# The order of ScalarE and VectorE through the first gate and value tile, written out by hand

## The chip, the cores and the metric

One core of a Trainium2 chip runs the kernel. The metric is the device time of one launch in microseconds: 483.07 us before the change (median of three runs, 482.94 to 483.83). Beside it stands one execution under the profiler, from which all rows below come.

## The reference

Attention with a soft cap over 24 heads, then two feed-forward layers, all in 32-bit floats. The change concerns the last layer, of which only the gate and value products matter here (x has 896 rows of 768 columns, both weights 768 by 1536):

```
def _moe2_ref(x, w_gate, w_val, w_out):
    g = x @ w_gate
    silu = g * (1.0 / (1.0 + np.exp(-g)))
    val = x @ w_val
    return (silu * val @ w_out).astype(np.float32)
```

The inputs arrive as 64-bit floats; the kernel makes 32-bit ones of them on the engines.

## The kernel before

**The work around the change.** The kernel computes attention, then the first feed-forward layer (its last products write the banks x), then the gate and value products, tile by tile of 128 columns of the weights (fc = 0 to 11), and last the output product (banks p). A full product is three matmuls of TensorE (PE): each 32-bit operand is split into a high and a low part, and high·high, high·low and low·high are added up (`mm3`). The helper `split` makes such a pair: ScalarE (ACT) copies the source into the high part (`hi_act`), VectorE (DVE) subtracts that from the source for the low part (`lo_dve`). So every split hands over from ACT to DVE.

**Tile 0** is computed directly by `ff2_gv`: four banks in turn, g and v for the first 384 rows of x, g and v for the other 512, each of 18 matmuls. ACT takes Silu of a g bank into ee, DVE multiplies it by the v bank and the result is split into buffers called a.

**Tiles 1 to 6** are computed by `ff2_gv_seven`, a scheme of Strassen's kind with seven products of half size (nine matmuls each). It needs sums and differences of weight halves and of quarters of x. Those of x are made once: four tiles T[0] to T[3], which the text calls T1 to T4, summed in xf and split into the buffer a (1344 columns each). Those of the weights are made for each tile by the steps that `sum_steps` returns: `sums` (the buffers t and wv), `first` (the split of wg into buffer g4[0], and then two subtractions in wg), `second` (two splits, of wv and t, into g4[2]), `third` (the split of the changed wg into g4[3] or g4[1]) and `fourth` (the split into w). Buffers g4 are called g in the rows, as is the PE's gate bank; 128x768 or 128x384 with source wg, wv or t is a weight buffer. For a tile, PE runs g, (in tile 1 also d), again g into the same bank, b, (c), again b into the same bank, c and e. Before PE adds into g or b again, ACT must have copied the first g product into ee, and DVE must have read the first b.

**The weights** of a tile come by DMA in 64-bit form (wg_raw, wv_raw, issued on SP) and are converted by `f32_shifted`: two ACTIVATEs on ACT, 768 columns each, then one SCALAR_TENSOR_TENSOR on DVE (called shift-and-or in this text). The converted floats wg and wv have two buffers in all, so the conversion for tile 2 waits until the last split of tile 1 has read them. The sums t and wv are made by DVE for tile 1 and by GpSimd (POOL) from tile 2 on.

**What sets the order.** A scheduler places the instructions of each engine, except on engines that stand in `pinned`, whose instructions keep the order in which the program writes them. PE is pinned all along, and ACT in tiles 1 to 6. In tile 0 of the kernel before, DVE is pinned for `sums` and `first`, ACT and DVE for `third`, DVE for what follows the loop (`second`, T3, `fourth`, T4), and ACT for the start of the conversion for tile 2. The rest is placed by the scheduler. On each engine an instruction that waits holds up all behind it.

**Names in the order.** g_2620, d_2635, b_2654, c_2666 and e_2696 are the PE banks of tile 1; g_384 and v_384 are those of tile 0's second half; a_2485 is the buffer of T1 to T4, a_2484 that of the split results of tile 0. wg_2492 and wv_2498 are the converted weights of tile 1. Those of tile 2 are wg_2612 and wv_2618 in the program before, wg_2607 and wv_2613 in the one after.

Of the kernel before, what the change touches and what calls it, by code (L numbers as in the profile page):

```python
# [5 lines left out]
F32 = mybir.dt.float32  # L6
# [4 lines left out]
AF = mybir.ActivationFunctionType  # L11
ALU = mybir.AluOpType
# [25 lines left out]
class Kernel:  # L38
# [562 lines left out]
    def load_gv(self, fc, i):  # L601
# [9 lines left out]
        self.hi_act(d[:, 0], f)  # L611
        self.lo_dve(d[:, 1], f, d[:, 0])

    def ff2_gv(self, fc, N, o):
        nc = self.nc
        ps = []
        for n, w in zip("gv", self.gvs[fc]):
            acc = self.pt.tile([128, 512], F32, name=f"{n}_{fc}_{o}", tag="m")[:, :N]
            for kk in range(self.KD):
                self.mm3(acc, (w[:, 0, kk, :], w[:, 1, kk, :]), [self.x2[kk][:, u, o:o + N] for u in range(2)],  # L620
                         kk == 0, kk == self.KD - 1)
            ps.append(acc)
        sg = self.sg[o > 0]
        self.A.activation(sg, ps[0], AF.Silu)
        first, k = fc < self.KD, fc % self.KD
        if o and first:
            n = self.HN
            self.V.tensor_tensor(self.S1f[:, k], ps[1][:, :n], sg[:, :n], op=ALU.mult)
            self.V.tensor_tensor(sg[:, n:], ps[1][:, n:], sg[:, n:], op=ALU.mult)
            self.V.tensor_tensor(self.S3f[:, k], self.sg[0], self.S1f[:, k], op=ALU.subtract)  # L630
            self.split(self.A61[k], sg[:, n:])
            return
        self.V.tensor_tensor(sg, ps[1], sg, op=ALU.mult)
        if o:
            self.V.tensor_tensor(self.S1f[:, k], self.S1f[:, k], sg[:, :self.HN], op=ALU.add)
        self.split((self.A22 if o else self.A11 if first else self.A12)[k], sg)

    def x_sub(self, t, c, a, z, p, m):

# [27 lines left out]
        self.x_sub(3, c, 384, 448, b[:, :64], t2[:, 384:])  # L667
        self.x_sub(2, c, 0, 448, t2, f)

    def x_split(self, i):  # L670

        self.split([self.T[i][:, u] for u in range(2)], self.xf[:, i])

    def sum_steps(self, fc):

        add, sub = ALU.add, ALU.subtract
        if fc > self.KD + 1:
            return (lambda: None,) * 5
        f = []
        for n, w in zip("gv", (self.w_gate, self.w_val)):  # L680
            src = w[:, fc * 128:(fc + 1) * 128].rearrange("(k p) f -> p k f", p=128)
            f.append(self.f32_shifted(self.load_shifted(src, f"w{n}_{fc}"), f"w{n}_{fc}", n == "v"))
        g, (v, rest) = f
        if fc > self.KD:
            d = [self.g4[m].rearrange("p (u x) -> p u x", u=2) for m in (2, 3)]

            def gate():
                self.split([d[0][:, u] for u in range(2)], g)

            def value():  # L690
                self.split([d[1][:, u] for u in range(2)], v)

            self.gvs[fc] = [t.rearrange("p u (k f) -> p u k f", f=128) for t in d]
            return rest, value, gate, lambda: None, lambda: None
        g, v = (t.rearrange("p (h x) -> p h x", h=2) for t in (g, v))
        s1 = self.t1
        pair = lambda t: [t.rearrange("p (h u x) -> p h u x", h=2, u=2)[:, :, u] for u in range(2)]
        t = self.gvs[fc] = [self.g4[0], self.g4[1 + fc % 2 * 2], self.g4[2], self.w1]
        S = self.G if fc > 1 else self.V

        def sums():
            rest()
            S.tensor_tensor(s1, v[:, 0], v[:, 1], op=add)
            S.tensor_tensor(v[:, 0], g[:, 0], v[:, 0], op=sub)

        def first():
            self.split(pair(t[0]), g)
            self.V.tensor_tensor(g[:, 0], s1, g[:, 0], op=sub)
            self.V.tensor_tensor(g[:, 1], g[:, 1], g[:, 0], op=sub)

        def second():
            hi, lo = pair(t[2])
            for m, x in enumerate((v[:, 0], s1)):
                self.split((hi[:, m], lo[:, m]), x)

        def third():
            self.split(pair(t[1]), g)

        def fourth():
            self.split([self.w1[:, u] for u in range(2)], v[:, 1])  # L720

        return sums, first, second, third, fourth

    def ff2_gv_seven(self, fc, steps):

        V, G, add, mult = self.V, self.G, ALU.add, ALU.mult
        n, k, ee = self.HN, fc % self.KD, self.ee
        a, s24, s31, a22 = self.gvs[fc]
# [10 lines left out]

        sg, c22, p1, u2 = (ee[:, 448 * m:448 * m + 448] for m in range(4))  # L740
        last = fc == self.KD
        sums, first, second, third, fourth = steps
        a = bank("g")
        product(a, A11, X(0, 0), True)
        self.A.activation(p1, a, AF.Copy)
# [1 line left out]
        if fc > 1:  # L747
            self.late()
        if last:
            first()  # L750
        if fc == 1:
            d = bank("d")
            product(d, S4, X(1, 1), True)
# [8 lines left out]
        else:  # L762
            product(a, A12, X(1, 0), False)
        if not last:
            first()
        self.A.activation(sg, a, AF.Silu)
        product(b, S3, T3, False)
        V.tensor_tensor(p1, p1, b, op=add)
# [1 line left out]
            c = bank("c")  # L770
            product(c, S1, T1, True)
        V.tensor_tensor(c22, p1, c, op=add)
        second()
        e = bank("e")
        product(e, A22, T4, True)
        V.tensor_tensor(p1, p1, e, op=add)
        third()
        fourth()
        if fc > 1:
            product(c, S4, X(1, 1), False)  # L780
        V.tensor_tensor(u2, u2, c, op=add)
# [10 lines left out]
        steps = self.sum_steps(fc + 2)  # L792
# [223 lines left out]
    def run(self):  # L1016
        nc = self.nc
        KD, K1, K2, F1 = self.KD, self.K1, self.K2, self.F1
# [16 lines left out]
        w = [self.w_in_steps(i) for i in range(KD)]  # L1035
        f, g, hi, lo = zip(*w)
        self.w_steps = [((), f[0][:1], ()), (f[0][1:2], (), f[0][2:] + g[0][:1]), ((), (g[0][1], hi[0]), (lo[0],))]
        for i in range(1, KD):
            a = g[i][:1]
# [41 lines left out]
        steps = h[1] + h[2][:1] + T[0] + h[2][1:] + h[3][:1] + T[1] + h[3][1:] + wo[0] + h[4][:2] + T[2] + h[4][2:] + wo[1] + h[5][:5] + T3 + h[5][5:] + h[6][:-1] + T4 + h[6][-1:]  # L1081
# [3 lines left out]
        n = self.HN = self.DM // 2  # L1085
        wb, gb = self.pool("wb"), self.pool("gb")
# [6 lines left out]
        steps = x2[0][0] + x2[0][1] + wo[2] + x2[1][0][:1] + T5 + x2[1][0][1:] + x2[1][1] + T6  # L1093
        steps += wo[3] + x2[2][0][:1] + x2[0][2] + x2[1][2] + [(0.0, lambda j=j: self.x_sums0(j)) for j in J[:2]]
        for j in range(2, KD):
# [4 lines left out]
            a, b = x2[j]  # L1100
# [26 lines left out]
        for fc in range(K2):  # L1127
            if 1 <= fc <= KD:
                self.pinned = (nc.tensor, nc.scalar)
                steps = self.ff2_gv_seven(fc, steps)  # L1130
                continue
            self.pinned = (nc.tensor,)
            if fc == KD + 1:
                w8 = self.w8 = wb.tile([128, 8, 2, n], F32R, name="w8", tag="w8")
                w = both(w8) + [(w1[:, 0], w1[:, 1])]
                w += [p for g in self.g4[:2] for p in both(g.rearrange("p (k u n) -> p k u n", k=2, u=2))]
                self.B11, self.B21 = w[4:10], w[:4] + w[10:12]
            for i, (N, o) in enumerate(((n, 0), (512, n))):
                if fc == 0:
                    if i == 0:  # L1140
                        sums, first, second, third, fourth = self.sum_steps(1)
                        self.pinned = (nc.tensor, nc.vector)
                        sums()
                        first()
                        self.pinned = (nc.tensor, nc.vector, nc.scalar)
                        third()
                        self.pinned = (nc.tensor,)
                    else:
                        self.x_split(1)
                        self.x_split(0)  # L1150
                elif fc + 1 < K2:
                    self.load_gv(fc + 1, i)
                elif i == 0:
                    self.load_w2(5)
                    self.load_w2(10)
                for c in early.get(fc, ())[i:i + 1]:
                    self.load_w2(c)
                self.ff2_gv(fc, N, o)
            if fc == 0:
                self.pinned = (nc.tensor, nc.vector)  # L1160
                second()
                self.x_split(2)
                fourth()
                self.x_split(3)
                self.pinned = (nc.tensor, nc.scalar)
                steps = self.sum_steps(2)


        self.pinned = ()
# [42 lines left out]
```

## Time and profile before

| | |
|---|---|
| median of three runs | 483.07 us (482.94 to 483.83) |
| the profiled execution | 480.33 us, its span 478.6 us |
| PE busy | 468.6 us (98%), 2988 matmuls |
| DVE busy | 375.2 us (78%) |
| ACT busy | 307.2 us (64%) |
| POOL busy | 42.8 us (9%) |

The profiled execution is 1.73 us longer than its span, and 2.74 us below the median of the timed runs. Times in rows count from the span's start. Tile 0 runs from 227.5 to 242, tile 1 from 242 to 258, tile 2 from there. A duration in a row overlaps the next row's start by some 0.1 us where instructions of one engine follow each other, so the step from start to start is what an instruction costs in a chain.

### The profile page before, as it was taken

The page shows a single profiled execution, that of the slowest core. Times are in us where ns is not written, and L with a number is a line of the kernel's source. Part 1 is how long each engine was busy: PE and PEld are TensorE (multiplying, and loading weights), DVE is VectorE, ACT ScalarE, POOL GpSimd, SP SyncE. Part 2 cuts the span into 40 slices and gives each one's busy share as a digit, 9 for nine tenths or more (in the row PEclk, how much of TensorE's full clock was granted, in tenths as well). Part 3 has the DMA queues.
Part 4 walks back from the last instruction along what each step waited for, and adds up shares of the span by engine and source line. Part 5 has one row for each costly group of instructions (what it writes and reads, how often), then busy time and mean ns, then how long its engine had stood idle before and what let it go on. Part 6 is the DMA issues. An engine that isn't in the chain of part 4 may idle for free. (4 is left out here: it accounts for less than half of the span.)

```text
span 478.6 us, 7682 instructions
## 1 busy us (share of the span) xinstructions
PE 468.6 (98%) x2988; PEld 386.7 (81%) x2988; DVE 375.2 (78%) x636; ACT 307.2 (64%) x445; POOL 42.8 (9%) x82
## 2 busy tenths in 40 slices
PE   9999999999999999999988999999999999999997
PEld 7445454538888899898977899999998899999996
DVE  3699999987769996765867888878566757999991
ACT  5999999931234798986944666678777746435220
POOL 1020101021000010000011333310000000000000
PEclk9999999999999999999999999999999999999999
DMA  6887575002000316365021444445666642010012
GB/s 179 185 210 165 133 189 147 21 2 88 0 1 12 120 45 198 96 195 167 3 71 62 132 132 131 132 131 162 198 206 213 210 133 66 1 66 2 18 58 90
DMA packets 65061, 52.33 MB, mean 109 GB/s; under 512 B 35585, under 2 KB 61953, under 8 KB 64257
## 3 DMA queue, kind: packets, MB, share of 16 engines
q1 hardware_dynamic: 64992, 51.85, 36.4%
q8 instruction: 23, 0.38, 0.3%
q14 instruction: 14, 0.11, 0.1%
q0 software_dynamic: 32, 0.00, 0.0%
HBM read 49.09 MB, written 2.75 MB: 108 GB/s over the span
## 5 line engine op out<-in xcount | busy, mean ns | idle before, releaser
L30 PE MATMUL g<-x,g 128*128 128x384 f32 (+2 forms) x324 | 69.6, 365 | 4.5 <-ACT ee L30 4.5
L30 PEld LDWEIGHTS g<-x,g 128*128 128x128 f32 x324 | 59.3, 188 | 11.3 <-ACT ee L30 5.3
L30 PE MATMUL h<-wi,x 128*128 128x512 f32 x252 | 59.1, 392 | 0.0
L30 PEld LDWEIGHTS h<-wi,x 128*128 128x128 f32 x252 | 46.8, 188 | 11.2 <-issue 1.5
L30 ACT ACTIVATE P<-sc,consts 112x896 f32<-112x896 f32 x48 | 45.4, 1009 | 4.0 <-PE sc L30 2.4
L30 PE MATMUL v<-x,g 128*128 128x384 f32 (+1 forms) x216 | 45.1, 362 | 0.0
L30 PEld LDWEIGHTS v<-x,g 128*128 128x128 f32 x216 | 39.1, 188 | 4.2
L30 ACT ACTIVATE P<-P,consts 112x3584 f32<-112x3584 f32 (+1 forms) x13 | 39.7, 3063 | 0.1
L30 PE MATMUL pv<-P,v 112*32 112x448 f32 x384 | 38.5, 540 | 0.0
L30 PEld LDWEIGHTS sc<-ks 64*112 64x112 f32 x288 | 23.4, 171 | 18.2 <-issue 7.7
L30 PE MATMUL sc<-ks 64*112 64x448 f32 x288 | 35.9, 379 | 0.2
L30 PE MATMUL x<-lB,wo 128*128 128x256 f32 (+1 forms) x192 | 35.2, 337 | 0.0
L30 PEld LDWEIGHTS x<-lB,wo 128*128 128x128 f32 x192 | 29.6, 189 | 3.4
L30 ACT ACTIVATE ee<-h,sms 128x512 f32<-128x512 f32 x14 | 9.5, 684 | 33.2 <-DVE sms L30 33.2
L30 PEld LDWEIGHTS pv<-P,v 112*32 112x32 f32 x384 | 12.2, 110 | 23.0 <-issue 20.7
L30 PE MATMUL x<-lA,wo 128*128 128x384 f32 x144 | 27.2, 338 | 0.0
L30 PE MATMUL p<-w,a 128*128 128x384 f32 x144 | 26.8, 334 | 0.0
L30 PEld LDWEIGHTS x<-lA,wo 128*128 128x128 f32 x144 | 25.2, 188 | 0.5
L30 PEld LDWEIGHTS p<-w,a 128*128 128x128 f32 x144 | 25.2, 188 | 0.1
L30 PE MATMUL b<-a,g 128*128 128x448 f32 x108 | 24.0, 366 | 0.7 <-DVE ee L30 0.7
L30 POOL COPY sm<-tr 32x14 f32<-32x14 f32 x48 | 14.9, 311 | 92.5 <-DVE tr L30 91.0
L30 PE MATMUL S<-P,ones 112*32 112x448 f32 x192 | 22.4, 549 | 0.0
(214 smaller groups left out, 905.8 us busy)
## 6 DMA issues: line engine op xcount, KB each, us to landing
wg_raw<-in_moe_w_gate_dram SPq DMA_DIRECT2D x12, 765.8 KB, 4.2
wv_raw<-in_moe_w_val_dram SPq DMA_DIRECT2D x11, 765.8 KB, 4.2
wi_raw<-in_moe_w_in_dram SPq DMA_DIRECT2D x6, 1024.0 KB, 6.6
w_raw<-in_moe_w_out_dram SPq DMA_DIRECT2D x6, 767.6 KB, 4.2
wo_raw<-in_moe_w_out_dram SPq DMA_DIRECT2D x6, 512.0 KB, 3.4
wo_raw<-in_moe_w_out_dram SPq DMA_DIRECT2D x6, 510.5 KB, 3.6
v<-in_v_dram SPq DMA_DIRECT2D x24, 112.0 KB, 3.5
kq<-in_k_dram SPq DMA_DIRECT2D x22, 112.0 KB, 2.7
```

The costliest lines, as they stand in the source:

```text
L30: i = f(*a, **k)
```

## The change

`ff2_gv` loses its special case for tile 0, and a new function `ff2_gv_first` writes out tile 0 with ACT and DVE pinned throughout. `sum_steps` now returns each split as two functions, one for ACT and one for DVE, so that the two engines' parts can stand apart in the program. The high and low parts of T1 to T4 (`x_hi`, `x_lo`), of the weights of tile 1, and the conversions for tile 2 get fixed places. From tile 1 on the functions are called in the order of before. The same instructions are issued, on the same engines. The order of PE's matmuls and that of SP's DMA issues are unchanged.

```diff
+    def gv_product(self, fc, i, N, o):
+
+        w = self.gvs[fc][i]
+        acc = self.pt.tile([128, 512], F32, name=f"{'gv'[i]}_{fc}_{o}", tag="m")[:, :N]
+        for kk in range(self.KD):
+            self.mm3(acc, (w[:, 0, kk, :], w[:, 1, kk, :]), [self.x2[kk][:, u, o:o + N] for u in range(2)],
+                     kk == 0, kk == self.KD - 1)
+        return acc
...
+    def x_hi(self, i):
+
+        self.hi_act(self.T[i][:, 0], self.xf[:, i])
+
+    def x_lo(self, i):
+
+        self.lo_dve(self.T[i][:, 1], self.xf[:, i], self.T[i][:, 0])
+
+    def ff2_gv_first(self):
+
+        V, n, mult, sub = self.V, self.HN, ALU.mult, ALU.subtract
+        nc = self.nc
+        sums, a, s2, s31, s24, a22 = self.sum_steps(1)
+        sums()
+        self.pinned = (nc.tensor, nc.vector, nc.scalar)
+        ga = self.gv_product(0, 0, n, 0)
+        self.x_hi(0)
+        a[0]()
+        a[1]()
+        self.x_lo(0)
+        self.x_hi(1)
+        va = self.gv_product(0, 1, n, 0)
+        sg, sb = self.sg
+        self.A.activation(sg, ga, AF.Silu)
+        s2()
+        self.x_hi(2)
+        s24[0]()
+        V.tensor_tensor(sg, va, sg, op=mult)
+        self.x_lo(1)
+        s24[1]()
+        gb = self.gv_product(0, 0, 512, n)
+        self.x_hi(3)
+        hi, lo = self.A11[0]
+        self.hi_act(hi, sg)
+        a22[0]()
+        self.x_lo(2)
+        self.lo_dve(lo, sg, hi)
+        for f in s31:
+            f()
+        self.A.activation(sb, gb, AF.Silu)
+        a22[1]()
+        self.x_lo(3)
+        vb = self.gv_product(0, 1, 512, n)
+        steps = self.sum_steps(2)
+        V.tensor_tensor(self.S1f[:, 0], vb[:, :n], sb[:, :n], op=mult)
+        V.tensor_tensor(sb[:, n:], vb[:, n:], sb[:, n:], op=mult)
+        V.tensor_tensor(self.S3f[:, 0], sg, self.S1f[:, 0], op=sub)
+        self.split(self.A61[0], sb[:, n:])
+        return steps
...
-        def first():
-            self.split(pair(t[0]), g)
+        def two(d, x):
+            return lambda: self.hi_act(d[0], x), lambda: self.lo_dve(d[1], x, d[0])
+
+        def s2():
             self.V.tensor_tensor(g[:, 0], s1, g[:, 0], op=sub)
             self.V.tensor_tensor(g[:, 1], g[:, 1], g[:, 0], op=sub)
 
-        def second():
-            hi, lo = pair(t[2])
-            for m, x in enumerate((v[:, 0], s1)):
-                self.split((hi[:, m], lo[:, m]), x)
-
-        def third():
-            self.split(pair(t[1]), g)
-
-        def fourth():
-            self.split([self.w1[:, u] for u in range(2)], v[:, 1])
-
-        return sums, first, second, third, fourth
+        hi, lo = pair(t[2])
+        s3, s1s = (two((hi[:, m], lo[:, m]), x) for m, x in enumerate((v[:, 0], s1)))
+        return (sums, two(pair(t[0]), g), s2, s3[:1] + s1s[:1] + s3[1:] + s1s[1:], two(pair(t[1]), g),
+                two([self.w1[:, u] for u in range(2)], v[:, 1]))
...
@@ in ff2_gv_seven @@
+        run = lambda fs: [f() for f in fs]
...
+            s2()
...
@@ in run @@
                 self.pinned = (nc.tensor, nc.scalar)
                 steps = self.ff2_gv_seven(fc, steps)
                 continue
+            if fc == 0:
+                steps = self.ff2_gv_first()
+                continue
             self.pinned = (nc.tensor,)
             if fc == KD + 1:
                 w8 = self.w8 = wb.tile([128, 8, 2, n], F32R, name="w8", tag="w8")
@@ -1136,19 +1177,7 @@
                 w += [p for g in self.g4[:2] for p in both(g.rearrange("p (k u n) -> p k u n", k=2, u=2))]
                 self.B11, self.B21 = w[4:10], w[:4] + w[10:12]
             for i, (N, o) in enumerate(((n, 0), (512, n))):
-                if fc == 0:
-                    if i == 0:
-                        sums, first, second, third, fourth = self.sum_steps(1)
-                        self.pinned = (nc.tensor, nc.vector)
-                        sums()
-                        first()
-                        self.pinned = (nc.tensor, nc.vector, nc.scalar)
-                        third()
-                        self.pinned = (nc.tensor,)
-                    else:
-                        self.x_split(1)
-                        self.x_split(0)
-                elif fc + 1 < K2:
+                if fc + 1 < K2:
                     self.load_gv(fc + 1, i)
                 elif i == 0:
                     self.load_w2(5)
@@ -1156,14 +1185,6 @@
                 for c in early.get(fc, ())[i:i + 1]:
                     self.load_w2(c)
                 self.ff2_gv(fc, N, o)
-            if fc == 0:
-                self.pinned = (nc.tensor, nc.vector)
-                second()
-                self.x_split(2)
-                fourth()
-                self.x_split(3)
-                self.pinned = (nc.tensor, nc.scalar)
-                steps = self.sum_steps(2)
 
 
         self.pinned = ()
```

On ACT, from the last splits of tile 0's weights to the first high part for tile 2. Before:

```order
L30 ACTIVATE g_3_1931<-wg_2492 128x2x384
L30 ACTIVATE ee<-g_384_2556 128x512
L30 ACTIVATE wg_2612<-wg_raw,consts 128x768
L30 ACTIVATE wg_2612<-wg_2612,consts 128x768
L30 ACTIVATE a_2484<-ee 128x128
L30 ACTIVATE wv_2618<-wv_raw,consts 128x768
L30 ACTIVATE ee<-g_2620 128x448
L30 ACTIVATE wv_2618<-wv_2618,consts 128x768
L30 ACTIVATE g_0_1928<-wg_2612 128x2x384
```

After:

```order
L30 ACTIVATE g_2_1930<-t_2489 128x384
L30 ACTIVATE ee<-g_384_2555 128x512
L30 ACTIVATE wg_2607<-wg_raw,consts 128x768
L30 ACTIVATE wg_2607<-wg_2607,consts 128x768
L30 ACTIVATE wv_2613<-wv_raw,consts 128x768
L30 ACTIVATE a_2484<-ee 128x128
L30 ACTIVATE ee<-g_2620 128x448
L30 ACTIVATE wv_2613<-wv_2613,consts 128x768
L30 ACTIVATE g_0_1928<-wg_2607 128x2x384
```

The first conversion of the value weights (wv from wv_raw) and the 128-wide high part of a_2484 have changed places; in both programs the copy of g_2620 stands behind the two. The high part of g_3 stands earlier now, ahead of the piece, and the one from t_2489 into g_2 just ahead of the Silu of bank g_384.

On DVE, from the end of the weight splits to the shift-and-or for the value weights. Before:

```order
L30 SCALAR_TENSOR_TENSOR wg_2612<-wg_raw,wg_2612 128x768
L30 TENSOR_TENSOR s_2486<-v_384_2575,ee 128x384
L30 TENSOR_TENSOR ee<-v_384_2575,ee 128x128
L30 TENSOR_TENSOR s_2487<-ee,s_2486 128x384
L30 TENSOR_TENSOR a_2484<-ee,a_2484 128x128
L30 TENSOR_TENSOR g_2_1930<-wv_2498,g_2_1930 128x384
L30 TENSOR_TENSOR g_2_1930<-t_2489,g_2_1930 128x384
L30 TENSOR_TENSOR a_2485<-xf,a_2485 128x1344
L30 TENSOR_TENSOR w_2488<-wv_2498,w_2488 128x384
L30 TENSOR_TENSOR a_2485<-xf,a_2485 128x1344
L30 SCALAR_TENSOR_TENSOR wv_2618<-wv_raw,wv_2618 128x768
```

After:

```order
L30 TENSOR_TENSOR g_2_1930<-wv_2498,g_2_1930 128x384
L30 TENSOR_TENSOR g_2_1930<-t_2489,g_2_1930 128x384
L30 TENSOR_TENSOR w_2488<-wv_2498,w_2488 128x384
L30 TENSOR_TENSOR a_2485<-xf,a_2485 128x1344
L30 SCALAR_TENSOR_TENSOR wg_2607<-wg_raw,wg_2607 128x768
L30 TENSOR_TENSOR s_2486<-v_384_2586,ee 128x384
L30 TENSOR_TENSOR ee<-v_384_2586,ee 128x128
L30 TENSOR_TENSOR s_2487<-ee,s_2486 128x384
L30 TENSOR_TENSOR a_2484<-ee,a_2484 128x128
L30 SCALAR_TENSOR_TENSOR wv_2613<-wv_raw,wv_2613 128x768
```

The two low parts into g_2, that of w_2488 and the two of 1344 columns (T3 and T4) stood behind the multiplications of bank v_384. They are ahead of them now, T3's earlier than the piece shows.

On DVE, in tile 1, from the low part of tile 2's first buffer to the second reading of bank b. Before:

```order
L30 TENSOR_TENSOR g_0_1928<-wg_2612,g_0_1928 128x2x384
L30 TENSOR_TENSOR wg_2612<-t_2489,wg_2612 128x384
L30 TENSOR_TENSOR wg_2612<-wg_2612 128x384
L30 TENSOR_TENSOR ee<-ee,b_2654 128x448
L30 TENSOR_TENSOR ee<-ee,d_2635 128x448
L30 TENSOR_TENSOR ee<-ee,b_2654 128x448
```

After:

```order
L30 TENSOR_TENSOR g_0_1928<-wg_2607,g_0_1928 128x2x384
L30 TENSOR_TENSOR ee<-ee,b_2654 128x448
L30 TENSOR_TENSOR wg_2607<-t_2489,wg_2607 128x384
L30 TENSOR_TENSOR ee<-ee,d_2635 128x448
L30 TENSOR_TENSOR wg_2607<-wg_2607 128x384
L30 TENSOR_TENSOR ee<-ee,b_2654 128x448
```

The first reading of b_2654 has moved from behind the two subtractions in wg to ahead of them; the reading of d_2635 stands between those.

## Rows read from the trace of the kernel before

**Rows 1.** The timeline of PE; start, duration, engine, line, operation, out<-in, [idle before, releaser]

```profile
241.95 1.99 PE L30 MATMUL g<-x,g 128*128 128x448 f32 x9
243.78 1.98 PE L30 MATMUL d<-x,g 128*128 128x448 f32 x9
247.96 2.09 PE L30 MATMUL g<-x,g 128*128 128x448 f32 x9 [2.20 <-ACT ee L30]
...
254.37 2.10 PE L30 MATMUL b<-a,g 128*128 128x448 f32 x9 [0.67 <-DVE ee L30]
256.31 1.99 PE L30 MATMUL e<-a,w 128*128 128x448 f32 x9
...
264.27 2.09 PE L30 MATMUL g<-x,g 128*128 128x448 f32 x9 [2.33 <-ACT ee L30]
```

**Rows 2.** The windows: stretch, length, busy time (instructions) per engine, clock, DMA

```profile
227.00:242.00 15.00, 15.00 (x76) 13.44 (x75) 11.06 (x16) 12.37 (x15) 0.00 (x0) 1.00 0.01 5
...
265.00:325.00 60.00, 60.00 (x298) 55.62 (x297) 50.82 (x87) 42.03 (x66) 18.11 (x17) 1.00 0.41 130
```

**Rows 3.** The timeline of ACT around the copies of bank g

```profile
246.49 1.00 ACT L30 ACTIVATE wv<-wv_raw,consts 128x768 f32<-128x768 int8 x1 [3.23 <-DVE w L30]
247.39 0.52 ACT L30 ACTIVATE ee<-g 128x448 f32<-128x448 f32 x1
247.81 0.92 ACT L30 ACTIVATE wv<-wv,consts 128x768 int32<-128x768 f32 x1
249.88 0.85 ACT L30 ACTIVATE g<-wg 128x768 fp32r<-128x768 f32 x1 [1.15 <-PE g L30]
...
260.04 1.01 ACT L30 ACTIVATE wg<-wg_raw,consts 128x768 f32<-128x768 int8 x1 [1.38 <-DVE g L30]
```

**Rows 4.** The timeline of DVE, from tile 0 to the first use of bank v

```profile
229.89 0.95 DVE L30 TENSOR_TENSOR g<-wg,g 128x768 fp32r<-128x768 f32 x1
230.75 1.55 DVE L30 TENSOR_TENSOR a<-xf,a 128x1344 fp32r<-128x1344 f32 x1
232.22 0.68 DVE L30 TENSOR_TENSOR xf<-x,xf 128x384 f32<-128x384 f32 x2
232.82 0.61 DVE L30 TENSOR_TENSOR xf<-xf 128x448 f32<-128x448 f32 x1
...
240.90 0.96 DVE L30 SCALAR_TENSOR_TENSOR wg<-wg_raw,wg 128x768 uint32<-128x768 uint32 x1 [2.02 <-ACT wg L30]
242.15 0.56 DVE L30 TENSOR_TENSOR s<-v,ee 128x384 f32<-128x384 f32 x1 [0.29 <-PE v L30]
242.63 0.28 DVE L30 TENSOR_TENSOR ee<-v,ee 128x128 f32<-128x128 f32 x1
...
245.90 0.55 DVE L30 TENSOR_TENSOR w<-wv,w 128x384 fp32r<-128x384 f32 x1
246.37 1.55 DVE L30 TENSOR_TENSOR a<-xf,a 128x1344 fp32r<-128x1344 f32 x1
```

**Rows 5.** The timeline of DVE, later: the readings in tile 1 and 2

```profile
252.63 0.56 DVE L30 TENSOR_TENSOR wg<-t,wg 128x384 f32<-128x384 f32 x1 [0.91 <-POOL wv L30]
...
256.51 0.62 DVE L30 TENSOR_TENSOR ee<-ee,b 128x448 f32<-128x448 f32 x1 [1.54 <-PE b L30]
...
267.08 1.26 DVE L30 TENSOR_TENSOR g<-wg,g 128x768 fp32r<-128x768 f32 x1 [0.45 <-ACT g L30]
```

**Rows 6.** The timeline of POOL, the sum and subtraction on the weights

```profile
250.90 1.70 POOL L30 TENSOR_TENSOR wv<-wg,wv 128x384 f32<-128x384 f32 x1
...
266.51 1.01 POOL L30 TENSOR_TENSOR t<-wv 128x384 f32<-128x384 f32 x1 [0.90 <-DVE wv L30]
```

**Rows 7.** The timeline of SP, one DMA issue

```profile
223.48 0.37 SPq L157 DMA_DIRECT2D wv_raw<-in_moe_w_val_dram  x1
```

**Rows 8.** The page's part 6: DMA issues, KB each, median us to landing

```profile
wv_raw<-in_moe_w_val_dram SPq DMA_DIRECT2D x11, 765.8 KB, 4.2
```

More of the change, by code (lines that the diff above doesn't have):

```diff
@@ L612, in load_gv @@
         self.lo_dve(d[:, 1], f, d[:, 0])
-    def ff2_gv(self, fc, N, o):
[L615 to L622, printed above, removed]
+    def gv_product(self, fc, i, N, o):
[5 more added lines that the diff above has]
+        return acc
+    def ff2_gv(self, fc, N, o):
+        ps = [self.gv_product(fc, i, N, o) for i in range(2)]
         sg = self.sg[o > 0]
         self.A.activation(sg, ps[0], AF.Silu)
[L625 to L632, printed above, removed]
+        k = fc % self.KD
         self.V.tensor_tensor(sg, ps[1], sg, op=ALU.mult)
@@ L635, in ff2_gv @@
             self.V.tensor_tensor(self.S1f[:, k], self.S1f[:, k], sg[:, :self.HN], op=ALU.add)
-        self.split((self.A22 if o else self.A11 if first else self.A12)[k], sg)
+        self.split((self.A22 if o else self.A12)[k], sg)
     def x_sub(self, t, c, a, z, p, m):
@@ L668, in x_sums @@
         self.x_sub(2, c, 0, 448, t2, f)
-    def x_split(self, i):
-        self.split([self.T[i][:, u] for u in range(2)], self.xf[:, i])
+    def x_hi(self, i):
[42 more added lines that the diff above has]
+        return steps
     def sum_steps(self, fc):
@@ L677, in sum_steps @@
         if fc > self.KD + 1:
-            return (lambda: None,) * 5
+            return (lambda: None,) * 6
         f = []
@@ L693, in sum_steps @@
             self.gvs[fc] = [t.rearrange("p u (k f) -> p u k f", f=128) for t in d]
-            return rest, value, gate, lambda: None, lambda: None
+            none = ()
+            return rest, (value,), lambda: None, (gate,), none, none
         g, v = (t.rearrange("p (h x) -> p h x", h=2) for t in (g, v))
@@ L741, in ff2_gv_seven @@
         last = fc == self.KD
-        sums, first, second, third, fourth = steps
+        sums, first, s2, second, third, fourth = steps
+        run = lambda fs: [f() for f in fs]
         a = bank("g")
@@ L749, in ff2_gv_seven @@
         if last:
-            first()
+            run(first)
         if fc == 1:
@@ L764, in ff2_gv_seven @@
         if not last:
-            first()
+            run(first)
+            s2()
         self.A.activation(sg, a, AF.Silu)
@@ L772, in ff2_gv_seven @@
         V.tensor_tensor(c22, p1, c, op=add)
-        second()
+        run(second)
         e = bank("e")
@@ L776, in ff2_gv_seven @@
         V.tensor_tensor(p1, p1, e, op=add)
-        third()
-        fourth()
+        run(third)
+        run(fourth)
         if fc > 1:
@@ L1138, in run @@
             for i, (N, o) in enumerate(((n, 0), (512, n))):
-                if fc == 0:
-                    if i == 0:
-                        sums, first, second, third, fourth = self.sum_steps(1)
-                        self.pinned = (nc.tensor, nc.vector)
-                        sums()
-                        first()
-                        self.pinned = (nc.tensor, nc.vector, nc.scalar)
-                        third()
-                        self.pinned = (nc.tensor,)
-                    else:
-                        self.x_split(1)
-                        self.x_split(0)
-                elif fc + 1 < K2:
+                if fc + 1 < K2:
                     self.load_gv(fc + 1, i)
@@ L1158, in run @@
                 self.ff2_gv(fc, N, o)
-            if fc == 0:
-                self.pinned = (nc.tensor, nc.vector)
-                second()
-                self.x_split(2)
-                fourth()
-                self.x_split(3)
-                self.pinned = (nc.tensor, nc.scalar)
-                steps = self.sum_steps(2)
         self.pinned = ()
```

## The prediction

> **What bounds the kernel now.** I read the clock row of the page first (its highest digit in all 40 slices), then the timeline of TensorE, then the windows, and last the timelines of ScalarE (ACT) and VectorE (DVE) around each hole. In the timeline the reader is to see that TensorE (PE) stands still three times in the part that the change touches: 2.20 us before the product g at 247.96, 0.67 before b at 254.37, 2.33 before g at 264.27 [rows 1]. From there on it is busy for 60.00 of 60.00 us, at a granted clock of 1.00 [rows 2]. So the end moves by what these three holes lose or gain, and by nothing else: what ACT or DVE save elsewhere lies beside a busy PE.
>
> *First hole.* PE waits for ACT's copy of bank g into ee, at 247.39. That copy stood behind the first conversion of the value weights (wv), which waited 3.23 us for DVE's w [rows 3]. DVE came to w (245.90 to 246.45) only after the multiplications of the last v bank, at 242.15, and what follows them [rows 4]. So the copy waits for work on weights that has nothing to do with the bank.
>
> *Second hole.* Product b at 254.37 adds into a bank that DVE must first have read. In the order of before that reading stands behind two subtractions in wg, the first of which waited for GpSimd (POOL), which ended its subtraction at 250.90 + 1.70 = 252.60; wg started at 252.63 [rows 5, 6]. POOL was late because the conversion of wv was late: again the first hole's cause.
>
> *Third hole.* ACT takes up the next weights at 260.04, after a wait of 1.38 us for DVE's g, and its second copy of a g bank stands behind that [rows 3]. DVE's work there starts with ee at 256.51, where it had waited 1.54 us for PE's product b [rows 5]. This hole therefore follows PE's own b by a fixed distance.
>
> **The change part by part.** No arithmetic is added or taken away. What moves:
>
> *DVE.* The low parts of tiles T3 and T4, the two g_2 and w come ahead of the last multiplications. I count from 229.89, where DVE in both programs has the same work behind it (there before starts g_0's low part [rows 4]). Three subtractions of x now stand first: two take 0.60 together (232.22 to 232.82), the third at most its 0.61 [rows 4]: 231.10. Then up to the multiplication s: two low parts of 768 columns at 0.86 (229.89 to 230.75) = 1.72; four of 1344 at 1.47 (230.75 to 232.22) = 5.88; seven instructions of 384 columns at 0.47 (245.90 to 246.37) = 3.29; one shift-and-or, the same size as the 768-wide parts, 0.86; 0.1 for one that reads what the one before it wrote, my choice [rows 4]. The sum is 11.85, so s starts at 242.95 instead of 242.15. It takes 0.48, the 128-wide product 0.28: ready at 243.71.
>
> *Is DVE held up in this chain?* ACT's load between 227 and 242 was 12.37 of 15 us [rows 2]. New in this stretch are one 768-wide high part (0.85) and the first conversion of wv (1.00) [rows 3]: 14.2, so ACT alone would be done by 241.2 and is ahead of DVE, which pays 1.47 for each tile. Where ACT must wait for a subtraction of DVE, DVE has a 1344-wide part to do meanwhile. I set the chain's waits to nothing; the ends are nothing and the 2.02 + 0.29 us that DVE idled in before at the shift-and-or and at s [rows 4]. The raw value weights were asked for at 223.48 [rows 7]; with the page's median of 4.2 us to landing [rows 8] they are there at 227.7, long before their conversion, which moves to about 241.
>
> *First hole after.* ACT's order is now: first conversion of wv, 128-wide high part, copy of g, second conversion. The high part starts at 243.71; at no more than the copy's 0.52 it ends by 244.25, and the copy by 244.77 [rows 3]. PE's g starts at 241.95 and d at 243.78, a step of 1.83 [rows 1], so PE wants the bank at 245.61. The slack is 0.8 us and the hole goes. From there PE goes on in steps of 1.83: b at 247.44, c at 249.27, the second b at 251.10, e at 252.93.
>
> *Second hole after.* The second conversion starts 0.42 after the copy (247.39 to 247.81) and takes 0.92 [rows 3]: 245.6. The shift-and-or of 0.96 [rows 4] ends at 246.6, POOL's sum (1.01) at 247.6, its subtraction (1.70) at 249.4 [rows 6]. DVE's reading of b now stands ahead of wg's subtractions and so no longer waits for POOL; ahead of it is g_0's low part. ACT's high part for that can start when PE leaves g, at 247.4, and takes 0.85 [rows 3]; DVE's low part runs from 248.3 beside POOL. Alone such an instruction took 0.95 [rows 4]; started while POOL's sum of 266.51 ran, it took 1.26 [rows 5, 6]. I take 1.26, the row with the same two neighbours: 249.6. The reading takes 0.62 [rows 5] and ends at 250.2, against the second b at 251.10. Slack 0.9, hole gone. The ends are 0.95 and a low part that starts only when POOL is through, at 249.4: then it ends at 250.35, the reading at 250.97, slack 0.1.
>
> The Trainium skill (SBUF — State Buffer, section "Who interferes with whom") says that a DVE instruction with two SBUF inputs contends with a GpSimd instruction that reads SBUF, and that the loser blocks for the whole instruction. The stretch of 1.26 beside POOL [rows 5, 6] is in its favour in kind; POOL's sum ended 0.44 after that start, so the row can't tell a whole wait from a slowdown. By the rule the late end of the sentence above holds, and PE would still find its bank read; with one more such collision it would not, which is the second rival.
>
> *Third hole after.* The order of DVE from its reading of the second b on, and of ACT from g_2 on, is the same as before, and both begin when that product ends; DVE is done with wg and d by about 251.8 (250.2 and three instructions of about 0.5) and waits there for PE as it did before. The hole stays at 2.33 us [rows 1]. The ends are 2.33 and nothing left of it.
>
> *Sum.* e started at 256.31 [rows 1] and starts at 252.93: 3.4 us (the idle time of two holes, 2.87; the rest is that the step into and out of a hole is longer: from d at 243.78 to g at 247.96 it is 4.18, which is 2.35 above 1.83 where the row counts 2.20 as idle). All behind it shifts. The profiled execution took 480.33 us with a span of 478.6; it becomes 476.9 with a span of 475.2. The three timed runs have a median of 483.07, which is 2.7 above the profiled one; the difference is carried over: 483.07 − 3.4 = **479.7**.
>
> **Rivals.**
> (1) Forecast: two holes go, the third stays. 479.7.
> (2) The reading of b is late, by collisions with POOL or a later conversion, and the second hole stays: 0.67 back, and some restart: 480.5. For it: the slack is 0.1 at the bad end. Against: the reading no longer stands behind the wait for POOL.
> (3) DVE keeps its idle 2.31 us in the longer chain: s starts at 245.3, 1.5 beyond the slack of 0.8, and the gain is 1.9: 481.2. Against it: that idle time came while T3, T4, g_2 and w lay ready behind the waiting instruction; now they fill it. If a further microsecond is lost, nothing that can be measured is left.
> (4) Slower. ACT and DVE, both fixed, hand over to each other in turns (ACT's g_3 waits for wg, DVE's g_3 for ACT, ACT's next conversion for DVE's g_3, the one of wv for DVE's w), and the copy stands behind all of it. Were the old 2.31 kept and a wait as long as the present 3.23 [rows 3] added, the copy would be 5.5 late, 4.7 beyond the slack, against 3.4 gained: 484.4. It decides from 4.2 us of lateness on. For it: nothing can step past a waiting instruction now. Against it: on each turn DVE has a ready 1344-wide part first.
> (5) The third hole goes as well, if the earlier weights reach ACT sooner: 5.7 us, 477.4. Against it: its chain starts at PE's own b.
>
> **How the numbers follow.** Chances: (1) 0.74, (2) 0.09, (3) 0.08, (4) 0.05, (5) 0.04. A measurement of this kernel can tell about 0.2%, 0.97 us, from no change. Faster by more: (1), (2), (5) and half of (3), 0.91; within: the other half of (3), 0.04; slower: 0.05. The range goes from 478.4, a microsecond below the forecast for the scatter of the median (482.94 to 483.83) and a part of (5), to 481.9, which takes in (2) and most of (3).
>
> **What would show it.** In the profile of the changed kernel: no idle time of PE before the second g product of tile 1 nor before its second b; e about 11.0 us after the start of the first g product of that tile (14.4 before); the 2.33 us before the third g still there; ACT's first conversion of wv waiting for nothing or little, and its high part of 128 columns for DVE instead, up to about 243.7; DVE without idle time over 0.3 us from 228 to 243. The forecast is wrong if PE still waits for the copy of g, if DVE's multiplication s starts after 243.8, or if the third hole has another length.

## The result, and the profile after

The changed kernel takes 478.38 us (median of four runs, 476.31 to 479.52) against 483.45 us for the kernel before (four runs, 482.94 to 483.92): a ratio of 0.9891, interval 0.9854 to 0.9927. That is 5.1 us less, where 3.4 were forecast (479.7, with a range from 478.4 to 481.9): the median lies 0.02 us below the range. With the five runs of a later measurement the changed kernel has nine, and their median is 478.53, inside it. The miss is therefore small; what follows asks why the time came out lower than 479.7 at all. The profiled execution, though, took 478.53 us with a span of 476.8, only 1.8 below the span before.

The timeline of PE in the changed kernel, columns as in [rows 1]:

```profile
242.04 1.99 PE L30 MATMUL g<-x,g 128*128 128x448 f32 x9
243.87 1.99 PE L30 MATMUL d<-x,g 128*128 128x448 f32 x9
245.69 1.99 PE L30 MATMUL g<-x,g 128*128 128x448 f32 x9
...
251.16 1.99 PE L30 MATMUL b<-a,g 128*128 128x448 f32 x9
252.99 1.99 PE L30 MATMUL e<-a,w 128*128 128x448 f32 x9
...
260.93 3.33 PE L30 MATMUL g<-x,g 128*128 128x448 f32 x9 [2.31 <-ACT ee L30]
264.06 2.34 PE L30 MATMUL b<-a,g 128*128 128x448 f32 x9
...
322.77 3.31 PE L30 MATMUL g<-x,g 128*128 128x384 f32 x18
```

Tile 1 starts 0.09 us later than in [rows 1]; with that taken off, e stands at 252.90 (forecast 252.93, before 256.31). The first two holes are gone, the third is there with 2.31 us. But the product behind it lasts 3.33 us instead of 2.09, and the next one 2.34 instead of 1.99. The windows of the same execution say why (stretch, length, busy time of PE, PEld, DVE, ACT and POOL, granted clock as a share of full speed, DMA):

```profile
260.00:261.00 1.00, 0.07 (x1) 0.07 (x1) 0.96 (x2) 1.00 (x3) 0.48 (x1) 1.00 0.21 51
261.00:262.00 1.00, 1.00 (x4) 0.93 (x5) 0.68 (x2) 0.90 (x2) 1.00 (x2) 0.71 0.78 254
262.00:263.00 1.00, 1.00 (x5) 0.88 (x4) 1.00 (x2) 0.00 (x0) 0.26 (x1) 0.50 1.07 376
263.00:264.00 1.00, 1.00 (x4) 0.92 (x3) 0.28 (x2) 0.07 (x1) 0.85 (x1) 0.50 0.30 103
264.00:265.00 1.00, 1.00 (x4) 0.88 (x4) 0.20 (x1) 1.00 (x2) 0.92 (x2) 0.59 0.71 173
265.00:266.00 1.00, 1.00 (x6) 0.93 (x6) 1.00 (x1) 0.20 (x1) 0.25 (x1) 1.00 1.06 360
```

PE stood still from 258.62; the clock was granted in full until about 0.5 us after it had started again, and then at half (1.2 GHz) for about 3.4 us. What is missing from full speed in these windows is 0.29 + 0.50 + 0.50 + 0.41 = 1.70 us. In the profiled execution of before the g product behind either long hole lasts 2.09 [rows 1], and no microsecond from 240 to 330 has a granted clock below 1.00.

ACT and DVE did what the working said. ACT around the copy, and DVE from w to the readings of b:

```profile
240.89 1.01 ACT L30 ACTIVATE wv<-wv_raw,consts 128x768 f32<-128x768 int8 x1
243.90 0.31 ACT L30 ACTIVATE a<-ee 128x128 fp32r<-128x128 f32 x1 [2.00 <-DVE ee L30]
244.12 0.53 ACT L30 ACTIVATE ee<-g 128x448 f32<-128x448 f32 x1
```

```profile
240.31 0.55 DVE L30 TENSOR_TENSOR w<-wv,w 128x384 fp32r<-128x384 f32 x1
240.78 1.55 DVE L30 TENSOR_TENSOR a<-xf,a 128x1344 fp32r<-128x1344 f32 x1
242.25 0.95 DVE L30 SCALAR_TENSOR_TENSOR wg<-wg_raw,wg 128x768 uint32<-128x768 uint32 x1
243.12 0.55 DVE L30 TENSOR_TENSOR s<-v,ee 128x384 f32<-128x384 f32 x1
...
248.39 1.07 DVE L30 TENSOR_TENSOR g<-wg,g 128x768 fp32r<-128x768 f32 x1 [1.93 <-ACT g L30]
249.54 0.62 DVE L30 TENSOR_TENSOR ee<-ee,b 128x448 f32<-128x448 f32 x1
...
253.19 0.62 DVE L30 TENSOR_TENSOR ee<-ee,b 128x448 f32<-128x448 f32 x1 [1.56 <-PE b L30]
```

The conversion of wv no longer waits for w (3.23 us in [rows 3]); the copy ends at 244.65, PE wants it at 245.69. DVE's chain has no idle time up to s at 243.12 (forecast 242.95). The first reading of b ends at 250.16 (forecast 250.2), one microsecond ahead of the second b. That this agrees so closely is partly luck: DVE was through with g_0's low part at 249.46, 0.1 earlier than forecast, and PE's first b, which the reading needs, ended at 249.49 (247.51 + 1.98).

**Two tables used below.** Each run of the experiments and of the changed kernel has its mean granted clock on record, so runs sort themselves into groups. A loss of 1.70 us in some 478 takes 0.004 off the mean, so 0.996 is read as one drop and 0.992 as two:

| | clock 0.998 to 1.000 | 0.995, 0.996 | 0.991 to 0.993 |
|---|---|---|---|
| before, 53 runs | 7 runs, median 480.61 | 19 runs, 481.93 | 27 runs, 483.86 |
| changed, 9 runs | 2 runs, 476.3 | 7 runs, 478.9 | none |

One more run of the kernel before, 487.63 at 0.986, was in the chip's slow state and is left out. The clock of the first runs of before, those of 483.07 and 483.45, is not on record.

And the time from the first g product of tile 1 to the first of tile 7 in each profile, which leaves out the scatter of the stages ahead (tile 1 starts between 241.28 and 242.56 in the eleven profiles):

| profile | us | clock drop inside |
|---|---|---|
| before (324.57 − 241.95) | 82.62 | no |
| changed (322.77 − 242.04) | 80.73 | one |
| changed, second profile (320.58 − 241.40) | 79.18 | no |

The row that ends this stretch in the profile of before, and the rows of the changed kernel's second profile (start, hole, end):

```profile
324.57 3.31 PE L30 MATMUL g<-x,g 128*128 128x384 f32 x18
```

```profile
241.40 1.99 PE L30 MATMUL g<-x,g 128*128 128x448 f32 x9
...
260.28 2.09 PE L30 MATMUL g<-x,g 128*128 128x448 f32 x9 [2.31 <-ACT ee L30]
...
320.58 3.29 PE L30 MATMUL g<-x,g 128*128 128x384 f32 x18
```

Without drops the change is worth 82.62 − 79.18 = 3.44 us; the drop costs 80.73 − 79.18 = 1.55.

### The profile page after: what moved, and what is told of

Same layout as the page of the kernel before. It is cut to its first block, busy times and chain, and to the rows that moved or that the text cites. A ratio compares the mean times of both kernels' runs of the same rounds, so it can differ in the third digit from the quotient of the medians.

```text
span 476.8 us, 7685 instructions
## 1 busy us (share of the span) xinstructions
PE 469.9 (99%) x2988; PEld 388.5 (81%) x2988; DVE 374.4 (79%) x636; ACT 306.6 (64%) x445; POOL 41.5 (9%) x82
## 4 chain that ended last, share of the span: by engine, by line
PE 97%; DVE 2%; ACT 0%; issue 0%; ACTq 0%
PE p L30 16%; PE g L30 14%; PE x L30 12%; PE h L30 12%; PE v L30 9%; PE pv L30 8%; PE sc L30 7%; PE S L30 4%; PE b L30 4%; PE c L30 4%; PE e L30 2%; PE lt L30 1%; PE T L30 1%; PE warm L30 1%; DVE ks L30 0%; DVE ee L30 0%
## 5 line engine op out<-in xcount | busy, mean ns | idle before, releaser
L30 PE MATMUL g<-x,g 128*128 128x384 f32 (+2 forms) x324 | 70.7, 369 | 2.3 <-ACT ee L30 2.3
L30 PEld LDWEIGHTS g<-x,g 128*128 128x128 f32 x324 | 60.3, 190 | 8.8 <-ACT ee L30 2.7
L30 ACT ACTIVATE g<-wg 128x768 fp32r<-128x768 f32 x18 | 15.2, 843 | 11.9 <-PE g L30 8.1
```

The source lines that it names most:

```text
L30: i = f(*a, **k)
```

## The experiments

Theory A: part of the 483.45 is time at half clock behind the long holes, and the change takes away a long hole and with it a drop. Theory B: only the holes count, and the 2.7 us between the median and the profile of before is a constant.

**Fill the two long holes of the kernel before.** The added product writes a bank that nothing reads.

```diff
         if fc == 1:
             d = bank("d")
             product(d, S4, X(1, 1), True)
+            product(bank('fill'), A11, X(0, 0), True)
             product(a, A12, X(1, 0), False)
...
+            if fc == 2:
+                product(bank('fill'), A11, X(0, 0), True)
             product(a, A12, X(1, 0), False)
```

> The kernel before, with one more product of nine matmuls (1.82 us, into a bank that nothing reads) put into the first and the third hole, where TensorE stands still for 2.20 and 2.33 us. Nothing waits for it and TensorE's next products start when they did. Theory A (the clock): the timed runs of the kernel before lose some 1.6 us behind each of the two long holes because TensorE's clock is granted at half for about 3 us there, and the profiled execution of before (480.33) was one that lost nothing. Then this kernel takes 480.3 to 480.6 in every run, at a clock of 1.00, about 3 us less than before. Theory B (only the holes count, and the profiled execution is shorter than the timed runs by a constant 2.7): no change, 483.4.

```profile
244.98 1.99 PE L30 MATMUL fill<-x,g 128*128 128x448 f32 x9
247.35 2.09 PE L30 MATMUL g<-x,g 128*128 128x448 f32 x9 [0.38 <-ACT ee L30]
...
252.92 1.99 PE L30 MATMUL b<-a,g 128*128 128x448 f32 x9
...
260.21 1.99 PE L30 MATMUL fill<-x,g 128*128 128x448 f32 x9
262.71 2.09 PE L30 MATMUL g<-x,g 128*128 128x448 f32 x9 [0.50 <-ACT ee L30]
```

Four runs, 478.78 to 479.75, median 479.14, all at 0.999 or 1.000; beside them the kernel before took 482.87 (ratio 0.9936, 0.9919 to 0.9954). More work, 3.7 us less time: theory B falls. It is lower than expected for a second reason, which the rows show: the second hole is gone too (no idle time before b at 252.92). That is worth 0.93 (tiles 1 to 6 take 81.69 us instead of 82.62), so 2.8 us are left that the holes' length does not explain. The scheduler had put DVE's reading of b ahead of wg's subtractions in this build, as in the changed kernel. So the second hole can go without an earlier wv; the reading's place is enough.

**Fill the one hole of the changed kernel**, by the second of these two insertions.

> The changed kernel with the same additional product of nine matmuls in the one hole that is left (2.31 us, tile 2). Theory A: the drop of the clock behind that hole goes, every run takes about 476.3 at a clock of 1.00 (that is the one of four runs of the changed kernel without a drop). Theory B: 478.4, as the changed kernel, with the same scatter.

```profile
258.50 1.99 PE L30 MATMUL fill<-x,g 128*128 128x448 f32 x9
260.98 2.09 PE L30 MATMUL g<-x,g 128*128 128x448 f32 x9 [0.49 <-ACT ee L30]
```

Four runs, 476.52 to 477.42, median 476.82, all at 0.998 to 1.000 (ratio to before 0.9889, 0.9871 to 0.9906). This is theory A's time and not B's.

**Move w's low part back, with T4's ahead of it.**

```diff
-        a22[1]()
-        self.x_lo(3)
...
         V.tensor_tensor(self.S3f[:, 0], sg, self.S1f[:, 0], op=sub)
+        self.x_lo(3)
+        a22[1]()
         self.split(self.A61[0], sb[:, n:])
```

> The changed kernel, with the low parts of T4 and of w moved back behind the three instructions on bank v_384; all else as in the changed kernel. Both theories expect the copy of bank g to wait again for the first conversion of wv and that for w: DVE reaches w at about 244.8, the copy ends at about 247.0, and TensorE stands still for 1.3 to 1.4 us before the second g product of tile 1, while the second hole stays away. Theory A: 477.7 where no clock drop follows either hole, 479.3 with one, 481 with two. Theory B: 479.8. If the first hole is not back, my account of its cause is wrong.

```profile
242.07 1.99 PE L30 MATMUL g<-x,g 128*128 128x448 f32 x9
...
247.12 2.09 PE L30 MATMUL g<-x,g 128*128 128x448 f32 x9 [1.25 <-ACT ee L30]
...
262.46 2.09 PE L30 MATMUL g<-x,g 128*128 128x448 f32 x9 [2.30 <-ACT ee L30]
...
323.71 3.29 PE L30 MATMUL g<-x,g 128*128 128x384 f32 x18
```

```profile
245.46 0.98 ACT L30 ACTIVATE wv<-wv_raw,consts 128x768 f32<-128x768 int8 x1 [4.62 <-DVE w L30]
```

The first hole is back: g starts 5.05 us after the tile's first product (247.12 − 242.07) instead of 3.65, which is 1.40 as worked out, and the conversion of wv waits for w again. Its cause stands. T4's low part, 1.47 us long, stands ahead of w here and adds to w's lateness; the run with T3 and T4 moved back behind w (below) tells the two apart. Ten runs: six at 0.999 or 1.000 with 478.83 to 479.67, four at 0.995 or 0.996 with 480.56 to 481.74, none below; ratio 0.9946 (0.9926 to 0.9966). The medians of the two groups, 479.24 and 481.38, lie 1.5 and 2.1 us above those expected: in the profile tiles 1 to 6 take 81.64 us, 1.06 more than 79.18 and 1.40 explain. The rows show where most of it goes. The scheduler's order in tile 2 is another in this build: DVE's reading of the second b (268.51) stands behind both subtractions in wg, the first of which waits 0.91 us for POOL. That is the second hole's order again, one tile on, and it costs PE 0.5 us before the next c and g products. From 301.39 to the end of tile 6 a product then takes 1.86 us from start to start instead of 1.82, at a granted clock of 1.00, another 0.4; why is not shown.

**Move T3's and T4's low parts back, but not w's.** `x_lo(2)` and `x_lo(3)` stand at the end of `ff2_gv_first`.

> The changed kernel, with only the low parts of T3 and T4 moved back behind the work on bank v_384; w and g_2 stay ahead of it. My account says that the weights' low parts alone remove the first hole: no idle time of TensorE before the second g of tile 1, and the same time as the changed kernel: 476.3 where the clock does not drop, 478.0 to 478.5 where it does. The rival, that T3 and T4 had to move as well, expects the conversion of wv to be late by up to 2.9 us and the second hole back, 0.7 us more or above.

```profile
246.98 0.95 DVE L30 SCALAR_TENSOR_TENSOR wv<-wv_raw,wv 128x768 uint32<-128x768 uint32 x1
248.84 0.99 DVE L30 TENSOR_TENSOR g<-wg,g 128x768 fp32r<-128x768 f32 x1 [0.92 <-ACT g L30]
249.99 0.62 DVE L30 TENSOR_TENSOR ee<-ee,b 128x448 f32<-128x448 f32 x1 [0.15 <-PE b L30]
```

PE has no idle time in tile 1; tiles 1 to 6 take 80.75 us (323.25 − 242.50) with one drop, against 80.73. Four runs, 478.19 to 479.85, median 478.71, all with one drop (ratio 0.9906, 0.9881 to 0.9932). Whether T3 and T4 stand ahead of the work on bank v_384 or behind it is worth nothing, as long as w is ahead; the weights' low parts are what counted.

**Take the third hole away in tile 2**, first attempt.

```diff
+        if fc == 2:
+            p1 = self.x00
...
+            if fc == 2:
+                c = bank("c")
+                product(c, S1, T1, True)
...
+        if fc == 1:
+            self.ahead = self.pt.tile([128, 512], F32, name="g_2", tag="m")[:, :448]
+            product(self.ahead, half(self.gvs[2][0], 0), X(0, 0), True)
+            self.A.activation(self.x00, self.ahead, AF.Copy)
         steps = self.sum_steps(fc + 2)
```

> The changed kernel, with the third hole attacked: in tile 2 alone, ScalarE's copy of bank g goes to a free buffer (the space of x00) and stands ahead of the next weights' conversions, and TensorE takes c ahead of the second b, whose bank is read later. Expected: TensorE goes from b straight to the second g (no 2.3 us), and stands still at most about 0.3 us before the second b. Theory A: with no long hole left no drop follows, 474.0 in every run at a clock of 1.00. Theory B: 478.4 less 2.2, 476.2.

```profile
258.91 1.99 PE L30 MATMUL g<-x,g 128*128 128x448 f32 x9
260.74 1.99 PE L30 MATMUL c<-a,g 128*128 128x448 f32 x9
263.03 2.09 PE L30 MATMUL b<-a,g 128*128 128x448 f32 x9 [0.30 <-DVE ee L30]
...
275.87 3.66 PE L30 MATMUL g<-x,g 128*128 128x448 f32 x9 [2.53 <-ACT ee L30]
```

The expected time was wrong. Tile 2 went as expected (0.30 us before b), and the hole came back in tile 3, 2.53 us long, with the clock drop behind it: 480.71 us (nine runs, 478.59 to 481.34; ratio 0.9952, 0.9931 to 0.9972). Three of the nine had no drop (0.998 to 1.000) and still took 478.59 to 479.54, so this kernel is slower than the changed one by more than the clock. DVE's low part for g_3 came after the sums in this order, ACT took up the next weights behind it, and the copy of tile 3 stands behind those:

```profile
271.63 1.00 ACT L30 ACTIVATE wg<-wg_raw,consts 128x768 f32<-128x768 int8 x1 [1.21 <-DVE g L30]
```

**Take it away in all tiles**, with the copy between two conversions and p1 and u2 of even tiles in the space of xf.

```diff
+        if fc % 2 == 0:
+            p1, u2 = self.xf[:, 0, 0], self.xf[:, 0, 1]
...
-        steps = self.sum_steps(fc + 2)
+        def ahead():
+            self.ahead = self.pt.tile([128, 512], F32, name=f"g_{fc + 1}", tag="m")[:, :448]
+            product(self.ahead, half(self.gvs[fc + 1][0], 0), X(0, 0), True)
+            self.A.activation(other[fc % 2 == 0], self.ahead, AF.Copy)
+
+        steps = self.sum_steps(fc + 2, ahead)
```

`sum_steps` calls `ahead` behind the conversion of wg.

> The changed kernel, with the third hole attacked another way, in all of tiles 2 to 6: ScalarE copies bank g of the next tile between the conversions of wg and wv, and the sums p1 and u2 of even tiles lie in the space of xf, so that neither the copy nor DVE's reading of b waits for what the tile before still reads. TensorE's order is unchanged. If the copy's place behind the conversion of wv, the split and the Silu was what held the third hole (theory C), about 0.7 us of it is left, no hole appears in tile 3, and the runs take 474.5 to 475.5 with no drop of the clock. If the chain through ACT, DVE and POOL that makes the next weights is the limit (theory D, as the early copy in tile 2 alone suggests), the idle time comes back in tile 3 or later and the runs take 477 or more.

PE's weight loads, with their idle time:

```profile
259.25 1.73 PEld L30 LDWEIGHTS g<-x,g 128*128 128x128 f32 x9 [0.92 <-ACT xf L30]
...
266.84 1.72 PEld L30 LDWEIGHTS c<-x,g 128*128 128x128 f32 x9 [0.27 <-DVE ee L30]
...
272.55 1.71 PEld L30 LDWEIGHTS g<-x,g 128*128 128x128 f32 x9 [0.35 <-ACT ee L30]
```

Each theory had a part right. The long hole shrank as C said (0.55 us of PE's idle time, 0.92 of the weight loads'), but short waits came up twice in each later tile, as D said, and the time is D's: tiles 1 to 6 take 79.54 us, a little more than 79.18. Yet all four runs kept the clock (1.00): 477.28 to 477.79, median 477.47, against 483.74 for before (0.9878, 0.9856 to 0.9900).

**The changed kernel once more.**

> The changed kernel once more, for more runs with the span and clock of each. Theory A (the clock) expects two groups: at a clock of 1.00 about 476.3 to 476.9, at 0.996 some 1.6 to 1.7 more, and none with two drops behind holes, since one hole is left; the kernel before has three groups (none, one, two drops). The theory that only the holes count expects one group with scatter that does not go with the clock.

476.34 at 1.00 and 478.38, 478.91, 479.00, 479.16 at 0.996 (ratio 0.9906, 0.9879 to 0.9933): two groups, as A said, though they lie 2.6 apart where 1.7 is the clock's; the rest is not explained. The profile is the one at 1.00; there g behind a hole of 2.31 us lasts its 2.09 us.

**The kernel before once more, and with the first hole alone filled.**

> The kernel before once more, for a profile of an execution in which the clock drops. Theory A (the clock): in two thirds of the executions or more the granted clock is at half for about 3 us right behind the first hole, the third, or both, and nowhere else behind tile 0; each costs about 1.6 us. Theory B expects a granted clock of 1.00 there, or drops that have nothing to do with the holes.

The expected drop is not in the profile: the profiled execution was again one without, so no trace of the kernel before shows where its drops lie. The ten runs (480.61 to 484.13) are in the table, in all three groups.

> The kernel before with the additional product of nine matmuls in the first hole alone; in this build DVE also reads the first b ahead of wg's subtractions, so the second hole should be gone (0.7 us), with wv's conversion as late as before. Theory A: two groups of runs, at a clock of 1.00 about 479 to 479.7 and at 0.996 about 1.6 more, and none at 0.992, since one long hole is left. Were the drops independent of the holes, the three groups of the kernel before would still be there.

This is the first of the two insertions alone. In its profile the first two holes are gone and the third is 2.32 us long. Ten runs, three at 0.999 or 1.000, seven at 0.996, none below: the clock's part holds. The times do not: 480.41 to 481.27 in the first group, 480.40 to 482.67 in the second, so that here a drop cost nothing that can be seen. Its profile, without a drop, needs 82.97 us for tiles 1 to 6, 1.28 more than that with both holes filled: DVE reads tile 2's second b behind a subtraction in wg here too, PE loses 0.4 us behind it, and from 279.03 on a product takes 1.86 us instead of 1.82 at a granted clock of 1.00, another 0.9. A PE that is late by a drop may simply not meet these losses. That was not tested.

**All runs by the number of long holes.** Kernels without an idle stretch over 0.55 us in tiles 1 to 6 (both fills, the copy taken early in all tiles): no drop in 12 runs. Kernels with one hole of 2.3 us or more (the changed kernel; w moved back, with a hole of 1.25 us besides; T3 and T4 moved back; the first early copy; the first hole filled): none in 14 runs, one in 28, two in none. The kernel before, with two: none in 7, one in 19, two in 27.

## Why the prediction was right in its rows and wrong in its number

- *The first hole* went, by the cause named: the low parts of T4 and w moved back bring it back with 1.40 us, those of T3 and T4 behind w do not.
- *The second hole* went. The first section called it the first hole's consequence; that was too much. With wv as late as before it also goes if DVE reads b first (the fill of the kernel before).
- *The third hole* kept its 2.31 us.
- *DVE's chain and ACT's waits*: within 0.2 us (s at 243.12 for 242.95, the high part at 243.90 for 243.71). *POOL's neighbourhood* was taken too dear: its subtraction took 1.01 instead of 1.70 and ended at 248.64, not 249.4, and the low part of g_0 beside it took 1.07, less than the 1.26 taken.
- *The sum*, 3.4 us: 3.44 between the two profiles without a drop.
- *The step that failed* is "the difference is carried over: 483.07 − 3.4", and with it "the end moves by what these three holes lose or gain, and by nothing else". The 2.7 us between the profile and the median were no constant. By the later runs they were time at half clock that the timed runs had and the profiled one had not: 46 of 53 runs of the kernel before have the clock of at least one drop, 27 that of two. With one long hole left no run of the changed kernel has two. So the median fell by the holes, 3.4, and by about one drop, 1.55 to 1.7: 5.0 to 5.1, as measured. That the sum fits to a tenth is luck: with four runs the interval of the result reaches from 3.5 to 7.1 us, and groups of like clock lie 4.3 us (no drop) and 3.0 us (one drop) apart, not 3.4. I had both numbers, 480.33 and 483.07, and explained neither.
- *The range* had no case for it: its lower end was made of scatter and the third hole. Of the rivals none came about; (4) and (3) needed a lateness of DVE that was not there.

That the kernel before loses its clock behind these very holes is shown by filling them, not by a trace of it.

## What to carry to other kernels

A hole of a busy TensorE has two prices, its length and the half-speed stretch that may follow; where the timed runs lie above the profiled one, look at the granted clock of every run before carrying the difference over. Work that nobody reads, put where TensorE would wait anyway, can be a gain: the changed kernel with its hole filled (476.82, four runs) lies below both kernels in the median, and so does the one with shorter waits (477.47); against the changed kernel this is not beyond the noise, as the intervals of their ratios to before overlap. Before moving a wait out of one tile of a pipeline, check that the chain that feeds the next tile is not the same length.

## What the hardware showed that was not expected

- The clock. Holes of 2.20 to 2.53 us went with half clock in most executions and not in all. In the three profiles that have a drop it stands behind such a hole, and the clock fell only after PE had begun again: 0.07 us after (first early copy), 0.5 (changed kernel) and 0.9 (T3 and T4 moved back). With no idle stretch over 0.55 us in that part (three kernels, twelve runs) no run was below 0.998. The Trainium skill (TensorE: Matmul & The Clock Gate, section "HAM oscillation — how this bites in real kernels") tells of such drops after waits in a loop over DMA, longer ones than these; here the wait is for another engine's copy.
- DVE beside POOL. In the profile of the first attempt on the third hole, one low part of 768 columns took 1.78 us instead of 0.95, with POOL's sum beside it:

```profile
264.23 1.78 DVE L30 TENSOR_TENSOR g<-wg,g 128x768 fp32r<-128x768 f32 x1
```

```profile
264.18 1.01 POOL L30 TENSOR_TENSOR t<-wv 128x384 f32<-128x384 f32 x1 [0.89 <-DVE wv L30]
```

  It ended 0.82 us after POOL's sum (266.01 − 265.19). The one of 1.26 in [rows 5, 6] ended 0.82 after POOL's too (268.34 − 267.52), and the one of 1.07 in the changed kernel 0.82 after POOL's subtraction, which ran from 247.63 to 248.64. The end is tied to the end of POOL's instruction, however much of it was left: 0.25 us, 0.44 or 0.96. So DVE waits for the whole of the other's instruction, as the Trainium skill says (SBUF — State Buffer, "Who interferes with whom"); the prediction had left that open. DVE's readings of b, which have one input in a PE bank, were not held up: 0.62 us at 261.32 in the changed kernel, with POOL busy from 261.25 to 262.26.
